# A hand-written instruction order of a retention and channel-mix kernel, replaced by another

## The chip, the cores and the metric

One core of one Trainium2 chip. The metric is the device time of one execution in microseconds (us). A run of the profiler gives, for one execution, every instruction of the five engines: TensorE (PE, with its weight loads as PEld), VectorE (DVE), ScalarE (ACT), GpSimd (POOL) and SyncE (SP).

## The reference

Inputs q, k, v of 4 batches x 8 heads x 768 tokens x 64, and a mixing layer with weights w_k (512 x 1024), w_v (1024 x 512), w_r (512 x 512) and vectors mu_k, mu_r. First a retention with decay, then the channel mix on its output:

```python
for t in range(S):
    state = gamma * state + outer(k[t], v[t])     # per batch and head, 64 x 64
    y[t] = scale * q[t] @ state
x = y, heads side by side                          # 4 x 768 x 512
xk = mu_k * x + (1 - mu_k) * x_prev                # x_prev: x one token earlier
xr = mu_r * x + (1 - mu_r) * x_prev
out = sigmoid(xr @ w_r) * (relu(xk @ w_k) ** 2 @ w_v)
```

## The kernel before, in words

The 3072 tokens are 12 blocks of 256, three to a batch: block n is part n % 3 of batch n // 3. For each block the kernel computes the retention in chunks, transposed, and puts the result in xT (512 features by tokens); then the channel mix of the block, or of two blocks together (GROUPS joins 3 with 4, 6 with 7 and 9 with 10).

A block is computed in one of three ways. Blocks in WIDE use two chunks of 128 tokens with full 128-row matmuls, blocks in HALF four chunks of 64 tokens in quarters of the array (64 x 64), and blocks 0 and 1 two chunks of 128 in pieces of 64 rows. Blocks in WHOLE transpose 128 x 64 pieces, the others 64 x 64 pieces.

Nothing schedules the program: the string ORDER is its order, on all engines at once. Each word is one step, `code.block.part`, with `~v`, `~a`, `~p`, `~s` naming the engine that does it (VectorE, ScalarE, GpSimd, SyncE) and `@` the PSUM banks that it uses. Each engine runs its own words in this order, one after the other, and waits for its inputs; so a word that waits holds up all later words of its engine. The words, in the order of a block:

- lq, lk, lv load q, k and v (lines 224 to 239). Those from `~p` are GpSimd's, which converts q and k to f16 on the way; the first halves of q and k of block 0 come from `~s` as f32 and are converted by cq and ck (cast, L248).
- vs scales v by the decay (scale_v, L254, instruction L255). Tq, Tk transpose q and k on TensorE (L274 whole, L280 in halves); Eq, Ek copy the result out of PSUM (copy, L243 on ScalarE).
- S are the scores (L320, L333, L341), M multiplies them by the mask on VectorE (L349, L356).
- C makes the state's increments (L368, L386, L397), U adds them up (L421, or a copy L245 for the first of a batch), G decays the state to the next block (L426 on ScalarE, L430 else).
- I and J bring the earlier state in (L443), Y the chunk's own tokens (L464, L480, L491), and D multiplies by gy, the powers of the decay, into xT (L509, L516).
- dx is the difference of neighbouring tokens (L531), X.n.w.j mixes 128 features for xk (w = 0) or xr (w = 1) (L560).
- K multiplies by w_k (L574 for two blocks, L584 for one), Qa and Qb are ReLU and square on ScalarE (L593, L601, L605), R multiplies by w_r (L614), s is the sigmoid (L620), V multiplies by w_v (L626, two words of four matmuls), O multiplies both into the output tile (L632), st stores it (L639).
- For the last 128 tokens of block 11, V, O and st come as Vc, Oc and sc in pieces of columns (L644, L651, L659).
- Once: gy.0 and gy.1 make the powers (L708 to L720), mu starts the loads of mu_k and mu_r on ScalarE's queue (load_mu, L676), mt transposes them on TensorE (L681), me copies them out on ScalarE (L684), wk, wr, wv load the weights in GpSimd's queue.
- z.n runs n units of matmuls on zeros that nobody reads, filler on TensorE: for each whole four units one f32 matmul (L693), for each one left over an f16 matmul of 512 columns (L700).

Tiles are in rings: 4 of q, k and v (f32 for v), 3 of most others, so a load also waits until its tile is free. GpSimd has at most eight loads under way.

Of the kernel before, what the change touches and what calls it, by code (L numbers as in the profile page):

```python
# [34 lines left out]
J.2 X.1.1.1 Qb.1.0 Qb.1.2 X.1.1.2 X.1.1.3 S.3.1@23 lv.4~p K.1.3@0 Qa.1.3 Qb.1.3 wv.0~p X.0.1.3
X.0.1.2 R.0.0@1 D.2~v dx.2~v X.2.0.2 Qb.0.1 s.0.0 X.2.0.0 lq.6~p R.0.1@6 s.0.1 Tk.4@0 X.2.0.3
R.1.1@7 X.2.0.1 vs.3~p M.3.0~v Ek.4~a K.2.3@1 Qa.2.3 K.2.0@6 Qa.2.0 M.3.1~v S.4.1@45 M.4.1~v
Tq.5@1 Eq.5~a C.3@23 U.3.0~v U.3.1 s.1.1 vs.4~v R.1.0@6 s.1.0 G.3~a K.2.1@0 I.3@45 Qb.2.3 S.4.0@23
M.4.0~v Y.3 C.4@67 U.4.0 U.4.1 G.4~a K.2.2@1 Qb.1.1 I.4@23 J.3 Qa.2.1 Qa.2.2 Y.4 Qb.2.0 D.3~v
V.0.0.0@6 Tq.6@45 J.4 dx.3~v V.1.1.0@7 D.4~v dx.4~v X.3.0.1 V.0.1.0@0 V.1.0.0@1 X.2.1.2 Qb.2.2  # L40
wv.1~p V.0.0.1 Eq.6~a V.0.1.1 lq.7~p lk.6~p Tk.6@45 Ek.6~a O.0.0 Tq.7@23 Eq.7~a V.1.0.1 S.6@45
lk.5~p Tk.5@6 X.3.0.2 X.3.0.3 X.3.0.0 K.3.3@2 Qb.2.1 K.3.2@3 O.1.0 Ek.5~a O.0.1 X.3.1.1 M.6~v
lv.5~p vs.5~v K.3.5@0 Qa.3.5 Qa.3.3 K.3.4@6 V.1.1.1 Qa.3.2 lv.6~p C.5@01 S.5@45 Qa.3.4 vs.6~v
C.6@23 Qb.3.3 Qb.3.2 O.1.1 M.5~v U.5.0 X.2.1.3 U.5.1 U.6.0~a U.6.1 U.6.2 U.5.2 U.6.3 K.3.0@6
X.2.1.1 Qa.3.0 Qb.3.0 V.2.0.0@7 K.3.6@4 Qa.3.6 K.3.7@6 st.0.1 Qa.3.7 Qb.3.7 I.5@01 I.6@45 V.2.0.1
K.3.1@3 Qa.3.1 Qb.3.1 X.2.1.0 R.2.0@6 lk.8~p Tk.8@23 lv.7~p Y.5 X.3.1.0 vs.7~v X.3.1.3 Y.6 X.3.1.2
s.2.0 R.3.1@6 D.5~v dx.5~v st.1.1 st.0.0 Ek.8~a X.5.0.3 O.2.0 X.5.0.0 V.2.1.0@2 X.5.0.1 R.3.0@3
D.6~v G.6~a Qb.3.4 s.3.0 s.3.1 lv.8~p R.2.1@0 s.2.1 X.5.1.3 X.5.0.2 R.4.0@1 s.4.0 V.2.1.1 lk.7~p
C.7@67 O.2.1 lk.9~p Tk.9@01 Ek.9~a lv.11~s Tk.7@45 Ek.7~a lq.8~p U.7.0 U.7.1 U.7.2 st.2.0 vs.8~v
K.5.1@3 dx.6~v Qa.5.1 K.5.2@2 I.7@45 S.7@01 U.7.3 K.5.0@6 M.7~v lv.9~p Qb.3.6 Qa.5.0 K.5.3@3  # L50
Qa.5.2 Qb.5.0 R.4.1@6 lk.11~p Qb.3.5 vs.9~v V.4.1.0@7 X.5.1.1 C.8@01 Y.7 D.7~v dx.7~v X.6.0.3
X.6.0.0 lq.11~p Qa.5.3 Qb.5.2 Tq.8@23 X.6.0.2 V.4.1.1 s.4.1 V.4.0.0@6 Eq.8~a V.3.1.0@2 Qb.5.3
Qb.5.1 V.4.0.1 X.6.0.1 lq.9~p G.7~a V.3.0.0@3 V.3.1.1 V.3.0.1 U.8.0 K.6.3@4 Qa.6.3 O.4.0 K.6.1@5
Qa.6.1 Qb.6.1 K.6.2@6 Qa.6.2 lq.10~p O.3.1 U.8.1 st.1.0 X.5.1.0 X.5.1.2 lk.10~p U.8.2 I.8@01 O.3.0
st.2.1 Tq.9@23 Eq.9~a O.4.1 Qb.6.3 S.8@45 M.8~v K.6.0@7 K.6.6@6 Qa.6.0 Qb.6.0 Qa.6.6 X.6.1.3
S.9@23 st.3.1 Tq.11@45 Y.8 Eq.11~a X.6.1.2 R.5.1@7 s.5.1 K.6.7@6 Qb.6.2 K.6.4@4 Qa.6.4 M.9~v D.8~v
dx.8~v X.8.0.0 X.8.0.3 X.8.0.1 X.8.1.1 V.5.0.0@5 R.5.0@7 K.6.5@4 s.5.0 X.6.1.1 Tk.10@01 Qa.6.7
lv.10~p vs.10~v X.6.1.0 C.9@23 U.9.0~v Ek.10~a st.3.0 Tq.10@67 V.5.0.1 O.5.0 X.8.0.2 V.5.1.0@0
R.6.1@1 Qa.6.5 U.9.1 U.9.2 U.9.3 Eq.10~a V.5.1.1 st.5.0 O.5.1 s.6.1 Qb.6.4 S.10@45 I.9@67 C.10@23
G.9~a vs.11~v U.10.0 U.10.1 U.10.2 Qb.6.5 M.10~v st.5.1 R.6.0@1 s.6.0 R.7.0@0 s.7.0 K.8.1@1 Qa.8.1  # L60
K.8.2@2 Qa.8.2 C.11@01 I.10@45 U.10.3 Y.9 K.8.0@3 D.9~v Qb.6.7 K.8.3@2 st.4.1 Tk.11@67 G.10~a
U.11.0 U.11.1 Qa.8.0 Ek.11~a U.11.2 Y.10 D.10~v R.7.1@3 s.7.1 dx.9~v dx.10~v X.9.1.1 I.11@01
X.8.1.0 S.11@67 M.11~v X.9.0.0 Qb.8.2 V.7.0.0@4 Qa.8.3 X.9.0.2 X.9.0.1 V.7.1.0@5 V.6.0.0@3 X.9.0.3
Qb.8.1 Qb.6.6 V.6.1.0@2 V.7.1.1 X.8.1.2 V.7.0.1 V.6.0.1 V.6.1.1 K.9.5@6 K.9.7@7 Qb.8.0 st.4.0
Qa.9.5 O.6.0 Y.11 O.7.1 X.8.1.3 R.8.1@6 D.11~v dx.11~v Qa.9.7 Qb.9.7 K.9.3@5 Qb.9.5 X.11.1.3
X.11.0.1 O.6.1 X.9.1.3 V.8.1.0@7 X.9.1.2 V.8.0.0@3 X.11.0.2 st.6.1 K.9.4@0 Qa.9.4 Qb.9.4 K.9.6@1
Qa.9.6 K.9.0@2 X.9.1.0 K.9.2@0 Qa.9.2 Qb.8.3 X.11.0.3 Qb.9.2 X.11.0.0 Qa.9.3 X.11.1.0 K.9.1@1
R.9.1@0 Qa.9.1 Qb.9.1 X.11.1.2 V.8.0.1 K.11.1@5 O.7.0 Qa.11.1 R.8.0@4 V.8.1.1 Qb.9.3 s.8.0
R.10.0@5 K.11.0@1 st.6.0 Qa.9.0 Qb.9.0 st.7.1 K.11.2@2 st.7.0 R.9.0@4 Qa.11.0 Qb.9.6 Qb.11.0
Qb.11.1 X.11.1.1 O.8.0 K.11.3@1 s.9.1 V.9.1.0@3 V.10.1.0@0 s.8.1 O.8.1 st.8.1 R.11.1@6 V.9.0.0@7  # L70
# [719 lines left out]
```

## Time and profile before

| | us |
|---|---|
| median of 3 runs | 156.06 (155.8 to 156.61) |
| the profiled execution | 156.68 |
| its span, first to last instruction | 154.9 |
| TensorE's first matmul starts | 1.05 |
| TensorE's last matmuls (L644 x8) start | 150.25 |
| the last store is issued | 151.78 |
| GpSimd scales v.1 (vs.1), v.3 (vs.3) | 11.00 for 1.94, 36.97 for 1.90 |

How to read the profile: busy time is given by engine; a line such as `L632 DVE ... x23 | 15.4, 683 | 14.5 <-ACT rs L620 7.4` is a group of 23 instructions of line 632 on VectorE, busy 15.4 us together, 683 ns each, before which the engine sat idle 14.5 us, 7.4 of it until a result of L620. In a timeline a row is start, busy time, engine, line, operation, tiles, shape and count, and in brackets the idle time before it with what ended it ("issue": nothing that the profile shows). The 40 slices give the busy share in tenths. TensorE's granted clock is 1.00 over the whole span by the core's view.

### The profile page before, as it was taken

The numbers are of one execution on the slowest core, as the hardware profiler recorded it, in microseconds if no ns is written. First come the engines' busy times: TensorE is split into PE (matmuls) and PEld (weight loads), VectorE is DVE, ScalarE is ACT, GpSimd is POOL, SyncE is SP. The second block draws the span as 40 slices with busy tenths as digits, with TensorE's granted clock in tenths as the row PEclk, the third lists the DMA queues.
The fourth block names the chain that finished last, engine by engine and source line by source line (L and its number), as shares of the span: only waits on it lengthen the run. The fifth ranks groups of instructions, "written<-read, shape, count | busy, mean of one in ns | idle before, by whom it ended". The sixth has DMA issues, their size and how long they took to land.

```text
span 154.9 us, 5520 instructions
## 1 busy us (share of the span) xinstructions
PE 146.0 (94%) x2423; PEld 83.9 (54%) x2423; DVE 126.9 (82%) x205; ACT 99.4 (64%) x186; POOL 55.5 (36%) x65
## 2 busy tenths in 40 slices
PE   7779799999999999999999999999999999999990
...
DVE  2588999999899999999999999998999998110541
...
DMA packets 45768, 22.31 MB, mean 144 GB/s; under 512 B 37416, under 2 KB 41392, under 8 KB 45744
## 3 DMA queue, kind: packets, MB, share of 16 engines
...
q8 instruction: 19, 0.31, 0.9%
...
## 4 chain that ended last, share of the span: by engine, by line
PE 55%; DVE 24%; DMA 12%; issue 4%; POOL 3%; DVEq 0%; POOLq 0%
PE ps L626 19%; DMA v<-in_v_dram 12%; PE ps L614 9%; PE ps L574 9%; PE ps L584 8%; DVE a L356 3%; DVE xk L560 3%; DVE xr L560 3%; DVE vs L255 3%; DVE dx L531 2%; DVE xT L516 2%; DVE tg L421 2%; DVE os L632 2%; PE ps L443 2%; DVE a L349 1%
## 5 line engine op out<-in xcount | busy, mean ns | idle before, releaser
L626 PE MATMUL ps<-wv,k2s 128*128 128x512 f16 x184 | 43.4, 379 | 0.0
L593 ACT ACTIVATE kr<-ps 128x512 f32<-128x512 f32 x48 | 27.8, 596 | 23.1 <-PE ps L574 18.0
L626 PEld LDWEIGHTS <-k2s 128*128 128x128 f16 x184 | 17.4, 98 | 20.0
L632 DVE SCALAR_TENSOR_TENSOR os<-ps,rs 128x512 f32<-128x512 f32 x23 | 15.4, 683 | 14.5 <-ACT rs L620 7.4
L614 PE MATMUL ps<-wr,xr 128*128 128x512 f16 x96 | 24.1, 380 | 0.0
L584 PE MATMUL ps<-xk,wk 128*128 128x256 f16 x192 | 24.0, 273 | 0.0
L232 POOL DMA_DIRECT2D k<-in_k_dram x20 | 17.7, 898 | 15.2 <-PE ps L280 10.5
L574 PE MATMUL ps<-xk,wk 128*128 128x512 f16 x96 | 22.5, 379 | 0.0
L584 PEld LDWEIGHTS <-wk 128*128 128x128 f16 x192 | 18.1, 98 | 4.9 <-DMA wk<-in_moe_w_k_dram 0.6
L620 ACT ACTIVATE rs<-ps 128x512 f32<-128x512 f32 x24 | 13.7, 594 | 9.3 <-PE ps L614 8.9
L560 DVE SCALAR_TENSOR_TENSOR xr<-dx,mu,xT 128x256 f16<-128x256 f32 (+1 forms) x36 | 19.2, 564 | 0.1
L560 DVE SCALAR_TENSOR_TENSOR xk<-dx,mu,xT 128x256 f16<-128x256 f32 (+1 forms) x36 | 18.8, 567 | 0.2
L232 POOL DMA_DIRECT2D v<-in_v_dram x18 | 16.2, 915 | 1.4 <-DMA q<-in_q_dram 0.5
L243 ACT COPY kT<-ps 128x1024 f16<-128x1024 f16 (+1 forms) x13 | 12.2, 947 | 5.2 <-PE ps L280 4.1
L601 ACT ACTIVATE k2s<-kr 128x512 f16<-128x512 f32 x24 | 14.9, 628 | 0.3
L574 PEld LDWEIGHTS <-wk 128*128 128x128 f16 x96 | 9.2, 98 | 10.8
L531 DVE TENSOR_TENSOR dx<-xT 128x1024 f32<-128x1024 f32 x12 | 14.6, 1223 | 0.3
L605 ACT ACTIVATE k2s<-kr 128x512 f16<-128x512 f32 x24 | 14.5, 628 | 0.1
L243 ACT COPY qT<-ps 128x1024 f16<-128x1024 f16 (+1 forms) x13 | 12.3, 949 | 2.4 <-PE ps L274 2.2
L614 PEld LDWEIGHTS <-xr 128*128 128x128 f16 x96 | 8.8, 97 | 9.2 <-DVE xr L560 0.2
L255 DVE TENSOR_TENSOR vs<-v,csm_sb 128x1024 f16<-128x1024 f32 x10 | 12.1, 1216 | 2.0 <-DMA v<-in_v_dram 2.0
L356 DVE TENSOR_TENSOR a<-ps,c_sb 128x1024 f16<-128x1024 f32 (+1 forms) x12 | 12.2, 1040 | 0.5 <-PE ps L333 0.4
...
## 6 DMA issues: line engine op xcount, KB each, us to landing
...
wk<-in_moe_w_k_dram POOLq DMA_DIRECT2D x2, 512.0 KB, 11.0
...
```

The costliest lines, as they stand in the source:

```text
L232: e.dma_start(out=dst[:, :, i * D : i * D + D], in_=src[:, i * P : i * P + P].rearrange("h p d -> p h d"),)
L243: e.copy(out=out, in_=in_)
L255: e.tensor_tensor(out=VS(n), in0=V32(n).rearrange("p h (i d) -> p i h d", i=2), in1=gks[:, int(half(n) or wide(n)), :, :, None].to_broadca ...
L356: nc.vector.tensor_tensor(out=a_full(n)[:, i, :, j0:j1], in0=pairs(banks("S", n, i, j0))[:, :, j0:j1], in1=(below if wide(n) else causal[: ...
L531: e.tensor_tensor(out=DX(k)[:, :, m * TM + t0 : m * TM + t1], in0=x[:, :, c + t0 : c + t1], in1=x[:, :, c - 1 + t0 : c - 1 + t1], op=ALU.s ...
L560: nc.vector.scalar_tensor_tensor(out=XM[w](k)[:, j, t0:t1], in0=DX(k)[:, j, t0:t1], scalar=mu[:, w * NCO + j : w * NCO + j + 1], in1=x[:, ...
L574: nc.tensor.matmul(banks("K", n, g), lhsT=wk16[:, co, g * P : g * P + P], rhs=XM[0](k)[:, co, :], start=(co == 0), stop=(co == NCO - 1),)
L584: nc.tensor.matmul(pz[:, i, :], lhsT=wk16[:, co, fo * P : fo * P + P], rhs=XM[0](k)[:, co, m * TM + t0 : m * TM + t1], start=(i == 0 and c ...
L593: nc.scalar.activation(out=kr, in_=banks("K", n, g, *u), func=AF.Relu)
L614: nc.tensor.matmul(banks("R", n, tb), lhsT=XM[1](k)[:, co, t : t + P], rhs=wr16[:, co, :], start=(co == 0), stop=(co == NCO - 1),)
L626: nc.tensor.matmul(banks("V", n, tb), lhsT=K2(n)[:, fo, tb * P : tb * P + P], rhs=wv16[:, fo, :], start=(fo == 0), stop=(fo == NFO - 1),)
L632: nc.vector.scalar_tensor_tensor(out=OS(2 * n + tb), in0=banks("V", n, tb), scalar=1.0 / (KSC * KSC), in1=RS(2 * n + tb), op0=ALU.mult, op ...
```

## The change

The constants and the whole order are replaced:

- block 5 leaves HALF and joins WIDE: 128-token chunks in place of 64-token ones; 64-token chunks are now used from block 6 on.
- all twelve vs are VectorE's; vs.1 and vs.3 were GpSimd's.
- U.0.0, U.3.0, U.9.0 and cq go from VectorE to ScalarE, G.7 from ScalarE to VectorE; all v loads are GpSimd's (lv.11 was SyncE's).
- the fillers are placed anew: before z.12, z.2, z.1, z.1, z.4, z.1, z.1; after z.3 four times ahead of the first transpose, then z.3, z.1, z.3, z.5, z.3, z.9.
- the first load on SyncE is k, then q (before: q, then k), the first on GpSimd half of k.0 (before: v.0). The words for mu come after cq on ScalarE.
- the last tile is cut in columns 256, 128 and 128 (CUTS) instead of 256 and 256; the order of the pieces is columns 256 to 383, then 0 to 255, then 384 to 511, the last stored from ScalarE's queue.

```diff
-HALF = (5, 6, 7, 8, 9, 10, 11)
+HALF = (6, 7, 8, 9, 10, 11)
...
-WIDE = (2, 3, 4)
+WIDE = (2, 3, 4, 5)
 HEADS = ((0, 1), (3, 2), (4, 5), (7, 6))
+CUTS = ((0, 256), (256, 384), (384, 512))
 ORDER = """
-lq.0.0.2~s gy.0 lv.0~p lk.0.0.2~s ck.0.0.2~v mu lk.0.2.4~p lq.0.2.4~p gy.1~a lv.1~p lk.1~p lq.1~p
-cq.0.0.2~v lq.2~p wk.0~p z.12@6 Tk.0.0.2@0 Tq.0.0.2@1 Ek.0.0.2~a Eq.0.0.2~a mt@2 wk.1~p vs.0~v
-z.2@6 S.0.0.0.2@01 me M.0.0.0.2~v S.0.1.0.2@45 Tk.0.2.4@2 M.0.1.0.2~v Tq.0.2.4@3 lk.2~p C.0@67
-U.0.0~v Ek.0.2.4~a Eq.0.2.4~a z.1@0 S.0.0.2.4@23 M.0.0.2.4~v I.0@45 S.0.1.2.4@01 M.0.1.2.4~v z.1@2
-Y.0 U.0.1 G.0~a vs.1~p Tk.1@7 Ek.1~a D.0~v dx.0~v lv.2~p lq.3~p lk.3~p C.1@01 U.1.0 X.0.0.0
-X.0.0.3 Tq.1@6 Eq.1~a z.4@2 S.1.1@67 lq.4~p X.0.0.2 I.1@45 Tq.2@0 M.1.1~v S.1.0@23 Eq.2~a wr~p
-X.0.0.1 z.1@7 K.0.0@6 M.1.0~v U.1.1 G.1~a lk.4~p Qa.0.0 X.0.1.0 X.0.1.1 Qb.0.0 Y.1 D.1~v dx.1~v
-X.1.0.1 z.1@3 K.0.3@7 X.1.0.2 Qa.0.3 K.0.2@1 X.1.0.0 Qa.0.2 X.1.0.3 Tk.2@6 K.0.1@0 Ek.2~a vs.2~v
-S.2.0@67 S.2.1@45 M.2.0~v Qb.0.3 K.1.1@1 K.1.2@2 Qa.0.1 Qb.0.2 lv.3~p C.2@0 Qa.1.2 Tq.3@3 Eq.3~a
...
-s.11.0 Oc.11.1.1 sc.11.1.1~a O.11.0 st.11.0 V.10.0.1 O.10.0 st.10.0 Vc.11.1.0@0 Oc.11.1.0
-sc.11.1.0~s
+lk.0.0.2~s lk.0.2.4~p gy.0 ck.0.0.2~v lq.0.0.2~s lv.0~p lq.0.2.4~p z.3@6 z.3@6 z.3@6 z.3@6
+Tk.0.0.2@0 Tk.0.2.4@1 vs.0~v cq.0.0.2~a Tq.0.0.2@2 lv.1~p mu Ek.0.0.2~a Eq.0.0.2~a z.3@6
+S.0.1.0.2@23 M.0.1.0.2~v Ek.0.2.4~a mt@0 me S.0.0.0.2@45 M.0.0.0.2~v Tq.0.2.4@1 C.0@67 Eq.0.2.4~a
+S.0.0.2.4@01 U.0.0~a I.0@23 M.0.0.2.4~v S.0.1.2.4@45 M.0.1.2.4~v vs.1~v z.1@0 Y.0 gy.1~a D.0~v
+U.0.1 lq.1~p Tq.1@6 Eq.1~a lk.1~p lk.2~p dx.0~v X.0.0.0 wk.0~p z.3@0 Tk.1@2 Ek.1~a X.0.0.2 X.0.0.1
+G.0~a X.0.0.3 z.5@0 Tk.2@2 X.0.1.2 C.1@67 Ek.2~a U.1.0 U.1.1 G.1~a S.1.1@45 M.1.1~v lv.2~p z.3@0
+I.1@23 S.1.0@01 M.1.0~v K.0.1@7 vs.2~v Qa.0.1 K.0.0@6 Y.1 wk.1~p z.9@4 K.0.3@7 K.0.2@0 Qa.0.0
+Qb.0.0 Qa.0.2 lq.2~p Tq.2@6 C.2@1 D.1~v dx.1~v Eq.2~a X.1.0.1 X.1.0.3 X.1.0.0 X.1.0.2 K.1.2@2
...
+st.9.1 s.11.0 st.9.0 Oc.11.1.1 st.10.1 sc.11.1.1~s V.11.0.1 O.11.0 st.11.0 Vc.11.1.0@7 Oc.11.1.0
+sc.11.1.0~s Vc.11.1.2@2 Oc.11.1.2 sc.11.1.2~a
 """
...
     def values_c(e, n, tb, c):
-        x = slice(c * dm // 2, (c + 1) * dm // 2)
+        x = slice(*CUTS[c])
```

The same line is replaced in result_c and store_c. The lines of the changed kernel stand one below those given here (CUTS adds a line).

More of the change, by code (lines that the diff above doesn't have):

```diff
@@ L35 @@
[L35 to L70, printed above, removed]
@@ L71 @@
-Qa.11.3 V.11.0.0@1 s.10.0 Qa.11.2 Qb.11.2 R.10.1@2 V.9.1.1 O.9.1 V.10.1.1 s.10.1 O.10.1 st.9.1
-Qb.11.3 V.9.0.1 st.10.1 s.11.1 Vc.11.1.1@2 s.9.0 V.10.0.0@6 O.9.0 R.11.0@0 V.11.0.1 st.8.0 st.9.0
-s.11.0 Oc.11.1.1 sc.11.1.1~a O.11.0 st.11.0 V.10.0.1 O.10.0 st.10.0 Vc.11.1.0@0 Oc.11.1.0
-sc.11.1.0~s
+lk.0.0.2~s lk.0.2.4~p gy.0 ck.0.0.2~v lq.0.0.2~s lv.0~p lq.0.2.4~p z.3@6 z.3@6 z.3@6 z.3@6
+Tk.0.0.2@0 Tk.0.2.4@1 vs.0~v cq.0.0.2~a Tq.0.0.2@2 lv.1~p mu Ek.0.0.2~a Eq.0.0.2~a z.3@6
+S.0.1.0.2@23 M.0.1.0.2~v Ek.0.2.4~a mt@0 me S.0.0.0.2@45 M.0.0.0.2~v Tq.0.2.4@1 C.0@67 Eq.0.2.4~a
@@ new lines @@
+S.0.0.2.4@01 U.0.0~a I.0@23 M.0.0.2.4~v S.0.1.2.4@45 M.0.1.2.4~v vs.1~v z.1@0 Y.0 gy.1~a D.0~v
[3 more added lines that the diff above has]
+Qb.0.0 Qa.0.2 lq.2~p Tq.2@6 C.2@1 D.1~v dx.1~v Eq.2~a X.1.0.1 X.1.0.3 X.1.0.0 X.1.0.2 K.1.2@2
+Qa.0.3 X.1.1.0 X.1.1.3 S.2.0@45 Qa.1.2 Qb.1.2 U.2.0 S.2.1@01 X.0.1.1 Qb.0.2 I.2@67 K.1.1@3 Qa.1.1
@@ new lines @@
+Qb.1.1 M.2.0~v lq.3~p K.1.0@2 lk.3~p Tk.3@4 M.2.1~v Y.2 Tq.3@3 Qb.0.1 Ek.3~a X.1.1.2 Eq.3~a wr~p
+J.2 X.0.1.0 X.0.1.3 R.0.1@5 Qa.1.0 X.1.1.1 Qb.0.3 D.2~v s.0.1 R.1.0@0 dx.2~v X.2.0.3 X.2.0.2
+lq.4~p lk.4~p X.2.0.1 S.3.0@67 X.2.0.0 s.1.0 S.3.1@23 M.3.1~v lv.3~p Tk.4@4 Ek.4~a Tq.4@1 Eq.4~a
+R.0.0@5 lk.5~p s.0.0 K.2.2@0 Qa.2.2 vs.3~v K.2.0@4 Qa.2.0 S.4.1@23 M.3.0~v Tk.5@5 Ek.5~a C.3@01
+U.3.0~a M.4.1~v K.1.3@4 lv.4~p R.1.1@6 Qb.1.0 s.1.1 U.3.1 lq.5~p Qa.1.3 vs.4~v I.3@23 S.4.0@01
+M.4.0~v K.2.3@5 G.3~a C.4@67 Tq.5@4 Qa.2.3 U.4.0 U.4.1 wv.0~p Y.3 lq.7~p Eq.5~a X.2.1.0 I.4@01 J.3
@@ new lines @@
+D.3~v Y.4 S.5.0@45 M.5.0~v wv.1~p Qb.1.3 V.1.0.0@7 Tq.7@23 lk.7~p dx.3~v G.4~a J.4 V.0.0.0@6 D.4~v
+dx.4~v Qb.2.2 Eq.7~a X.3.0.3 X.3.0.1 K.2.1@4 X.3.0.0 V.0.1.0@5 V.1.0.1 O.1.0 V.0.1.1 X.3.0.2 O.0.1
+Qa.2.1 Qb.2.1 V.1.1.0@4 Tk.7@01 Ek.7~a lq.6~p lv.5~p Tq.6@23 Eq.6~a vs.5~v V.0.0.1 O.0.0 V.1.1.1
+K.3.4@7 Qa.3.4 X.2.1.1 lk.6~p K.3.6@0 lv.6~p Qa.3.6 X.2.1.3 C.5@5 Qb.2.0 Tk.6@23 Ek.6~a Qb.3.6
+S.5.1@67 U.5.0 X.2.1.2 K.3.5@1 O.1.1 R.2.0@5 Qb.2.3 K.3.0@0 M.5.1~v I.5@23 vs.6~v s.2.0 Qa.3.5
+Qa.3.0 S.6@67 S.7@45 M.7~v M.6~v Y.5 K.3.3@1 C.6@45 U.6.0~a U.6.1 Qb.3.5 Qa.3.3 Qb.3.3 lv.7~p J.5
@@ new lines @@
+vs.7~v K.3.7@0 U.6.2 D.5~v lv.9~p U.6.3 K.3.1@6 Qa.3.1 dx.5~v Qa.3.7 lq.8~p X.5.0.2 X.5.0.1 Qb.3.7
+st.0.1 R.2.1@7 lq.9~p lk.10~p s.2.1 X.5.0.0 K.3.2@1 Qa.3.2 st.1.1 V.2.0.0@4 G.6~a X.5.0.3 I.6@23
+C.7@67 lv.8~p U.7.0 U.7.1 Tq.8@01 Eq.8~a X.3.1.1 Qb.3.4 Qb.3.2 U.7.2 V.2.1.0@5 V.2.0.1 lk.9~p
+st.0.0 O.2.0 K.5.2@0 Qa.5.2 U.7.3 V.2.1.1 Qb.5.2 I.7@01 O.2.1 st.2.1 K.5.3@6 K.5.1@4 Qb.3.0 Qb.3.1
+V.4.0.0@5 X.3.1.3 X.5.1.1 lv.10~p Qa.5.3 Qb.5.3 Qa.5.1 Tk.9@67 Ek.9~a lk.8~p Y.7 st.2.0 Y.6
+X.3.1.0 X.3.1.2 R.4.0@4 R.4.1@6 s.4.1 vs.8~v V.4.0.1 D.6~v D.7~v V.3.1.0@7 s.4.0 O.4.0 dx.6~v
```

24 lines of the change are left out of this document (22 added, 2 removed).

## The prediction

> **What bounds the kernel now.** I read the page's busy shares first, then its 40 slices, then TensorE's timeline, then VectorE's, each with what ended the idle time.
>
> ```profile
> PE 146.0 (94%) x2423; PEld 83.9 (54%) x2423; DVE 126.9 (82%) x205; ACT 99.4 (64%) x186; POOL 55.5 (36%) x65
> ...
> PE   7779799999999999999999999999999999999990
> ...
> DVE  2588999999899999999999999998999998110541
> ```
>
> PE is full from the eleventh slice to the last; it ends at 151.3, and 3.6 us of last result, store and closing follow. VectorE is full from slice three until about 131 us. So the end is TensorE's work plus the waits between 1.05 us (its first instruction) and 151.3. VectorE sets the pace of the start, where TensorE can only do what VectorE has made.
>
> The timeline of TensorE (start, busy, line, count, idle before and its releaser):
>
> ```profile
> 7.58 0.20 PE L681 MATMUL ps<-csm_sb,mu 8*128 8x8 f32 x1 [0.84 <-DMA mu<-in_moe_mu_r_dram]
> ...
> 15.59 0.35 PE L341 MATMUL ps<-qT,kT 64*64 64x128 f16 x10
> 16.29 0.30 PE L341 MATMUL ps<-qT,kT 64*64 64x128 f16 x6 [0.34 <-issue]
> ...
> 18.42 1.10 PE L584 MATMUL ps<-xk,wk 128*128 128x256 f16 x8
> 19.73 0.64 PE L491 MATMUL ps<-a,vs 64*64 64x128 f16 x32 [0.21 <-DVE a L356]
> ...
> 24.79 1.95 PE L584 MATMUL ps<-xk,wk 128*128 128x256 f16 x16
> ...
> 27.75 0.31 PE L443 MATMUL ps<-qT,tg 64*64 64x128 f16 x8 [0.33 <-DVE tg L421]
> ...
> 38.92 0.44 PE L386 MATMUL ps<-vs,k 128*64 128x64 f16 x16 [0.52 <-POOL vs L255]
> ```
>
> The second pair is the wait for instructions that the change is after: S.1.1 is one group of 16 with one input, it stops after ten, and nothing releases it. It costs about 0.55 us. Queue q8 (instruction) shows 19 packets and 0.31 MB for 2 x 2423 TensorE instructions, that is 256 instructions a packet; I find no second stop inside a group that only such a packet explains. So at most 0.6 us is to be had from it.
>
> **Spacings.** Start to start, from the timeline and the chain of waits: 0.216 us for a 512-column matmul (4 in 0.86), 0.109 for 256 columns (8 in 0.87), 0.57 for a whole transpose word (16), 0.27 for a half one (32), 0.33 for a wide scores word of 8 with its change of shape; going from dense to small work adds 0.09, back again 0.12 to 0.15. Counting both orders word by word with these gives, from the first K.1 word (24.79 us now) to the last matmul, 124.3 us of work now. Measured are 126.5; the 2.2 left over are waits, the largest 0.4 at 27.75, 0.6 at 38.92, 0.3 at 58.1 and 0.3 at 75.1. The count is good to 0.2 us.
>
> **Part 1, filler.** The z words hold 22 units now and 36 after. Now they last 5.1 (z.12, at the slow first clock, 0.85 a pass), 1.1 (z.4) and 6 x 0.216: 7.5 us. After: four z.3 ahead of the first transpose, which at the same slow rate are again about 5.1; 12 units at 0.216, 2.6; three of the f32 kind in z.5 and z.9 at 1.06 (z.4's row), 3.2. Together 10.9, or 3.4 us more TensorE time. Filler is free where TensorE would have waited anyway, so the start has to be followed on VectorE.
>
> **Part 2, VectorE's start.** Its timeline now:
>
> ```profile
> 8.16 1.23 DVE L255 TENSOR_TENSOR vs<-v,csm_sb 128x1024 f16<-128x1024 f32 x1 [2.00 <-DMA v<-in_v_dram]
> ...
> 13.02 1.23 DVE L516 TENSOR_TENSOR xT<-ps,gy_sb 128x1024 f32<-128x1024 f32 x1 [0.52 <-PE ps L443]
> ...
> 20.91 1.23 DVE L516 TENSOR_TENSOR xT<-ps,gy_sb 128x1024 f32<-128x1024 f32 x1
> ```
>
> D.0 starts at 13.02 and D.1 at 20.91. After, POOL issues half of k.0 ahead of v.0; k's landing now follows v's by about 0.4 (Tk.0.2.4 starts at 8.61, vs.0 at 8.16), so v.0 comes 0.4 later and vs.0 starts near 8.6. Four half masks (0.6 each) follow, and then vs.1 (1.13), which was POOL's (1.94 at 11.00): D.0 at 8.6 + 1.13 + 2.4 + 1.13 + 0.2 = 13.45 at the earliest, even though U.0.0 (0.4) goes to ScalarE.
>
> From D.0 to the end of M.1.0 VectorE does D.0 1.26, two U before the masks and one after D.0 at 0.335 each, dx 1.26, five X at 0.395, two masks 2.26: 7.8 us, against 6.7 now, where one U and one X come later. So Y.1 is at 21.3 at the earliest, against 19.73. TensorE has its fillers, Tq.1, Tk.1, Tk.2, C.1 and two K.0 words in that time and waits little; two K.0 words are done by Y.1 instead of one.
>
> From Y.1 to the first K.1 word TensorE needs 5.6 us: Y.1 0.6, z.9 2.4, two K.0, Tq.2, C.2. VectorE's vs.2, D.1, dx.1 and four X need 5.3 in parallel. So z.9 costs only 0.3; without it the X would be waited for. First K.1 word: 26.9 at the earliest.
>
> **Part 3, mu.** Now ScalarE issues both mu loads in its first 2.6 us:
>
> ```profile
> 1.73 0.58 ACTq L676 DMA_DIRECT2D mu<-in_moe_mu_k_dram  x1
> 2.34 0.27 ACTq L676 DMA_DIRECT2D mu<-in_moe_mu_r_dram  x1
> ```
>
> mt (L681) still waited until 7.5: 5.1 us from the second issue. After, cq.0 is a ScalarE copy ahead of them, waiting for q from SP (now second on SP; SP's second load was in by 5.2, when ck started). So the second mu issue is at about 5.85. mt stands in TensorE's order behind S.0.1.0.2, near 9, and everything queued behind it waits: S.0.0.0.2, Tq.0.2.4 and C.0, and on ScalarE, behind me, Eq.0.2.4, without which the last two scores, their masks, vs.1 and D.0 don't come. From mt to M.0.0.2.4 I count 1.75 us (S 0.3, T 0.25, 0.2 to ScalarE, copy 0.6, S and its change 0.3, 0.1); VectorE is free for that mask at 10.9. So mu is harmless up to 9.2 and costs VectorE a microsecond for each one after.
>
> The latency at this time is not shown. Nearest rows: the page's csm_sb load on the same queue 2.4 us, mu itself 5.1, a v load on SP's queue among others 6.4; so mu is in between 8.3 and 12.3. I start from mu's own row and take 0.7 off, since c_sb (issued at 1.19, 3.2 to landing) stood ahead of it on ScalarE's queue until 4.4: 4.4 us, mu in at 10.2, loss 1.0, range 0 to 3.1.
>
> [...]
>
> So the first K.1 word is at 27.9.
>
> **Part 4, the rest.** From there the new order holds 124.9 us: 0.35 more because S.2 (0.65) comes after that point and C.2 (0.3) before it, 0.2 because block 5 in 128-token chunks has dearer scores (16 x 27 ns for 32 x 8.5) and dearer intra matmuls, the rest shape changes. VectorE's whole load grows by about 1.4 us: vs.1 and vs.3 +2.26, second mask of block 5 +1.13, G.7 +0.34, against cq 0.4, three U to ScalarE 1.0, two U and a split D of block 5 0.9. That is hidden: I laid VectorE's sum beside TensorE's sum from 28 us on; the closest K, R, I, Y or C word has its input 0.4 us early, most over 1. So the waits of now (2.2) should go, POOL's scaling at 38.92 among them; I leave 0.3, between 0 and 1.2, for copies on ScalarE.
>
> Last tile: Vc pieces of 256, 128, 128 columns in place of 256, 256. 16 matmuls of 128 columns are not in the trace; bounds are half of 0.109 (no change) and 0.109 itself (+0.85); I take +0.2, as nearer to half, since weight loads (98 ns) overlap in the 256-column row. [...] The last result covers 128 columns: 0.29 (the 128-column row of gy_sb) for 0.42, and half the bytes: -0.2 (0 to -0.4).
>
> **Sum.** Last matmul: 27.9 + 124.9 + 0.3 + 0.2 = 153.3, against 151.3: +2.0; tail -0.2; so +1.8. The profiled run took 156.68 (span 154.9), so 158.5; the median of the runs is 156.06, 0.6 lower, so **157.9** beside it. 0.5%, or 0.8 us, is about what a measurement of this kernel can tell from no change.
>
> **Rivals** (times beside the median).
> 1. **mu in time (chance 0.25: within 0.5%).** A small load needs 2.4 us as csm_sb did, and mt waits for nothing. Then the first K.1 word is at 26.9 and the time 156.9; with no late waits and 128 columns at half of 256, 156.4. For it: csm_sb's row. Against: mu's own. [...]
> 2. **More than one wait for instructions (0.17: faster).** The waits view puts some 8 us of TensorE's weight loads down to "issue" (L280 1.5, L341 1.3, L491 1.1, L368 1.1 and so on). I took them for changes of shape, which the new order has as often (79 against 80). If those before 45 us are instructions that come late, the new order, which has fewer instructions in front of each packet and filler between, saves up to 1.5 of them; with mu in time that is 157.9 - 1.0 - 1.5 = 155.4. It decides if the gaps at changes of shape shrink by half before 45 us. Against: the same idle of 0.42 stands before L280 at 45.38 and 50.29, where TensorE's own loss is only 0.09.
> 3. **VectorE waits for v.3 (0.08: slower).** POOL now idles 3.6 us before its scaling of v.3, which starts at 36.97 when v.3 lands. VectorE is in order; its vs.3 is due near 38. If v.3 comes after 39.2 (C.3 has 1.2 to spare), each microsecond is lost: 2 us late beyond that, 160.
>
> That the instruction wait stays is inside the range (0.55).
>
> Forecast 0.50: 157.0 to 159.4 on its own. With the rivals the range is **155.3 to 160.0**; about a tenth is left out at each end. Faster 0.17, same 0.25, slower 0.58.
>
> **What would show it.** Right: L681 released by mu after 9.5; D.0 after 13.5 and D.1 after 22.3; the first K.1 word after 27; TensorE's waits after 28 us under 1; no stop inside a scores group. Wrong: D.1 before 22, or waits for DVE or ACT of over 1 us after 30; then the end follows those and not this sum.

## The result, and the profile after

The changed kernel takes 160.12 us in the median of four runs (159.96 to 161.51), the kernel before on the same chip 156.28 (155.80 to 156.61): a ratio of 1.026, 95% interval 1.021 to 1.031. Slower was forecast, at 157.9 us; the time is 2.2 us above that and just outside the range. The profiled execution took 161.51 us, span 159.7; it is the slowest of the four, the others lie between 159.96 and 160.17. (Executions over 1.5% above the fastest of their kernel are left out of every ratio but not out of the medians, so the two can differ a little.)

The page of the changed kernel: busy time, then the 40 slices of some 4 us each. The clock's row is new here, since it stood at 9 throughout before.

```profile
PE 150.9 (94%) x2383; PEld 85.9 (54%) x2383; DVE 128.1 (80%) x203; ACT 100.2 (63%) x186; POOL 53.5 (34%) x65
...
PE   7928999999999999989999998999999999999992
...
DVE  2367969999999999998978999999999999120252
...
PEclk9995599999999999999999999999999999999999
```

TensorE's third slice is nearly empty (a 2), and right behind it two slices run at half the granted clock (the two 5s). TensorE is busy 4.9 us longer than before with 40 instructions fewer: longer filler in part, a lower clock for the rest. In the eighteenth slice (67.9 to 71.9 us, an 8) it stops once more.

TensorE's timeline of the start, then VectorE's, then what ScalarE's queue issued for mu:

```profile
10.87 0.20 PE L682 MATMUL ps<-csm_sb,mu 8*128 8x8 f32 x1 [2.82 <-DMA mu<-in_moe_mu_r_dram]
...
15.30 1.07 PE L275 MATMUL ps<-c_sb,q 128*64 128x128 f16 x16
...
20.30 0.64 PE L275 MATMUL ps<-c_sb,k 128*64 128x128 f16 x16
...
21.14 0.40 PE L342 MATMUL ps<-qT,kT 64*64 64x128 f16 x16
...
24.73 0.64 PE L492 MATMUL ps<-a,vs 64*64 64x128 f16 x32
...
29.98 1.05 PE L585 MATMUL ps<-xk,wk 128*128 128x256 f16 x8
```

```profile
8.16 1.23 DVE L256 TENSOR_TENSOR vs<-v,csm_sb 128x1024 f16<-128x1024 f32 x1 [2.85 <-DMA v<-in_v_dram]
...
11.35 0.69 DVE L357 TENSOR_TENSOR a<-ps,c_sb 128x512 f16<-128x512 f32 x1 [1.37 <-PE ps L342]
...
15.47 1.23 DVE L517 TENSOR_TENSOR xT<-ps,gy_sb 128x1024 f32<-128x1024 f32 x1 [0.30 <-issue]
...
25.72 1.22 DVE L517 TENSOR_TENSOR xT<-ps,gy_sb 128x1024 f32<-128x1024 f32 x1
```

```profile
5.13 0.55 ACTq L677 DMA_DIRECT2D mu<-in_moe_mu_k_dram  x1
5.70 0.27 ACTq L677 DMA_DIRECT2D mu<-in_moe_mu_r_dram  x1
```

Read them together. mt (L682) waits for mu until 10.87; mu's second load was issued at 5.70, so it was 5.17 us from issue to use (5.24 in the kernel before, 2.34 to 7.58). VectorE's second mask (11.35) waited for the scores queued behind mt, so D.0 starts at 15.47 in place of 13.02, D.1 at 25.72 in place of 20.91, and the first K.1 word at 29.98 in place of 24.79. The two transpose rows are the clock: 16 transposes take 1.07 us at 15.30 and 0.64 at 20.30. The scores word S.1.1 (21.14), which stopped after ten before, is now one piece of 16: the stop that the change was after has gone from there. (That it was a wait for instructions is the author's reading; the row of before shows 0.34 us that nothing releases.) The new order need not be the reason, since two variants of the old order below (only mu, or only mt and me moved) don't show that stop either.

The windows view puts numbers to it: a stretch, its length, then busy time of PE, PEld, DVE, ACT and POOL with counts, granted clock, DMA share, GB/s.

```profile
9.18:12.59 3.41, 1.42 (x57) 1.03 (x57) 1.50 (x3) 1.07 (x4) 2.53 (x3) 1.00 1.81 179
12.59:16.00 3.41, 3.14 (x67) 2.32 (x65) 2.95 (x4) 1.12 (x4) 2.43 (x3) 0.50 1.70 193
16.00:19.42 3.42, 3.42 (x28) 1.73 (x25) 3.38 (x7) 1.64 (x2) 1.69 (x3) 0.50 1.14 250
19.42:22.83 3.41, 3.41 (x96) 1.80 (x95) 2.11 (x6) 2.74 (x8) 1.92 (x3) 1.00 1.57 190
```

TensorE worked 1.42 us of the first stretch, and the next two, 6.83 us together, were granted half the clock. In the profile of before the clock is never halved inside the span (mean 1.000; after, 0.978).

After 28 us there is one stop of the kind that the change was to remove, inside the group of 32 C matmuls of block 7:

```profile
70.62 0.38 PE L369 MATMUL ps<-vs,k 64*64 64x64 f16 x20
71.66 0.28 PE L369 MATMUL ps<-vs,k 64*64 64x64 f16 x9 [0.66 <-issue]
```

Three of the 32 ran just ahead, among those of the word before; nothing releases the 24th. That is 0.66 us of idle time, about 0.85 against the spacing of the others.

### The profile page after: what moved, and what is told of

Read it like the earlier page. It is cut to its first block, busy times and chain, and to the rows that moved or that the text cites. A ratio compares the mean times of both kernels' runs of the same rounds, so it can differ in the third digit from the quotient of the medians.

```text
span 159.7 us, 5450 instructions
## 1 busy us (share of the span) xinstructions
PE 150.9 (94%) x2383; PEld 85.9 (54%) x2383; DVE 128.1 (80%) x203; ACT 100.2 (63%) x186; POOL 53.5 (34%) x65
## 4 chain that ended last, share of the span: by engine, by line
PE 84%; DVE 6%; DMA 6%; issue 1%; ACT 1%; SPq 0%; DVEq 0%
PE ps L627 25%; PE ps L615 13%; PE ps L585 13%; PE ps L575 11%; PE ps L275 4%; DMA mu<-in_moe_mu_r_dram 3%; DMA k2s<-in_q_dram 2%; PE ps L444 2%; PE ps L281 2%; PE ps L694 2%; PE ps L334 2%; PE ps L701 2%; DVE a L357 1%; DVE xr L561 1%; PE ps L481 1%
## 5 line engine op out<-in xcount | busy, mean ns | idle before, releaser
L627 PE MATMUL ps<-wv,k2s 128*128 128x512 f16 x184 | 44.4, 379 | 0.0
L575 PE MATMUL ps<-xk,wk 128*128 128x512 f16 x96 | 23.4, 379 | 0.0
L233 POOL DMA_DIRECT2D v<-in_v_dram x20 | 18.1, 937 | 9.4 <-DVE vs L256 6.7
L256 DVE TENSOR_TENSOR vs<-v,csm_sb 128x1024 f16<-128x1024 f32 x12 | 14.6, 1219 | 2.9 <-DMA v<-in_v_dram 2.9
L357 DVE TENSOR_TENSOR a<-ps,c_sb 128x1024 f16<-128x1024 f32 (+1 forms) x14 | 14.6, 1067 | 2.1 <-PE ps L342 2.1
## 6 DMA issues: line engine op xcount, KB each, us to landing
wv<-in_moe_w_v_dram POOLq DMA_DIRECT2D x2, 512.0 KB, 10.2
```

The source lines that it names most:

```text
L233: e.dma_start(out=dst[:, :, i * D : i * D + D], in_=src[:, i * P : i * P + P].rearrange("h p d -> p h d"),)
L256: e.tensor_tensor(out=VS(n), in0=V32(n).rearrange("p h (i d) -> p i h d", i=2), in1=gks[:, int(half(n) or wide(n)), :, :, None].to_broadca ...
L357: nc.vector.tensor_tensor(out=a_full(n)[:, i, :, j0:j1], in0=pairs(banks("S", n, i, j0))[:, :, j0:j1], in1=(below if wide(n) else causal[: ...
L575: nc.tensor.matmul(banks("K", n, g), lhsT=wk16[:, co, g * P : g * P + P], rhs=XM[0](k)[:, co, :], start=(co == 0), stop=(co == NCO - 1),)
L627: nc.tensor.matmul(banks("V", n, tb), lhsT=K2(n)[:, fo, tb * P : tb * P + P], rhs=wv16[:, fo, :], start=(fo == 0), stop=(fo == NFO - 1),)
```

## The experiments

Theory A, after the result: all of the loss comes from mt. It stands early in TensorE's order, mu comes 5.2 us after a late issue, and this costs twice, once because VectorE's masks come late (about 2 us) and once because 3 us of idle TensorE halve its clock for 6.8 us (about 1.5 us). Rivals: B, the new order with its extra VectorE work and filler is slower by itself; C, the clock has nothing to do with it.

**mu early.** The changed kernel with the two loads of mu issued ahead of the casts.

```diff
-lk.0.0.2~s lk.0.2.4~p gy.0 ck.0.0.2~v
+lk.0.0.2~s lk.0.2.4~p gy.0 mu ck.0.0.2~v
...
-Tq.0.0.2@2 lv.1~p mu Ek.0.0.2~a
+Tq.0.0.2@2 lv.1~p Ek.0.0.2~a
```

> The changed kernel with one word moved: mu is issued as ScalarE's first own word, as it was before, and no longer behind cq.0. Theory A (mu's late issue holds TensorE for 3 us at mt, and that idle time is what halves the granted clock from 12.6 to 19.4 us): mt is released before 8.5, the clock stays 1.0, D.0 starts at 13.5, the first K.1 word at 27, the median near 157.0 (3 us less than 160.1). Rival B (VectorE's longer list decides, the start of it does not matter): D.0 earlier, but the end within 0.8 us of 160.1. Rival C (the clock falls for another reason, such as too little work in the first 12 us whatever mt does): the clock is halved again in about the same stretch, median 158.5 or more.

Measured: 156.38 us median (155.39 to 158.09, ten runs), ratio to before 0.9985 (0.995 to 1.002). TensorE's timeline:

```profile
7.88 0.22 PE L682 MATMUL ps<-csm_sb,mu 8*128 8x8 f32 x1
...
26.78 1.05 PE L585 MATMUL ps<-xk,wk 128*128 128x256 f16 x8
```

mt starts at 7.88 and waits for nothing; D.0 is at 12.87, the first K.1 word at 26.78. The clock was not full in this profile: its mean over the 154.9 us is 0.989, which is 3.4 us at half, and 16 transposes take 1.07 us at 12.69. The five runs with a mean clock of 0.997 or more took 155.4 to 156.4. So where mu is issued is worth 3.7 us, and B in its strong form is out.

**The same delay put into the kernel before.** Only the word mu moves, behind gy.1.

```diff
-ck.0.0.2~v mu lk.0.2.4~p lq.0.2.4~p gy.1~a lv.1~p
+ck.0.0.2~v lk.0.2.4~p lq.0.2.4~p gy.1~a mu lv.1~p
```

> The kernel before with one word moved: mu is issued on ScalarE behind gy.1, at about 5.5 us and not at 1.7. Theory A: mu lands near 10.8, mt holds TensorE from 6.5 on, over 4 us, the clock is halved for a window of 6.8 us after it, D.0 starts at 15 to 15.5, and the median is 159 to 161 (3 to 5 us more than before). Rival B (an early loss is made good later because TensorE's queue has slack): within 1 us of 156.3. Rival C (the clock fell in the changed kernel for its other fillers): no halved clock here, +2 us.

Measured: 161.42 us (160.94 to 163.72, four runs), ratio 1.033 (1.028 to 1.038). TensorE's timeline, and the windows view as above:

```profile
11.21 0.24 PE L681 MATMUL ps<-csm_sb,mu 8*128 8x8 f32 x1 [4.22 <-DMA mu<-in_moe_mu_r_dram]
```

```profile
6.16:9.57 3.41, 0.82 (x17) 0.48 (x16) 1.23 (x1) 1.55 (x4) 3.41 (x5) 1.00 1.38 251
9.57:12.99 3.42, 1.78 (x21) 0.78 (x23) 0.10 (x1) 0.17 (x1) 3.11 (x4) 0.50 1.75 183
```

The late mu alone makes the old order as slow as the new one, without any of the other edits. With the longer idle of 4.2 us (6.99 to 11.21) come three halved stretches, 10.24 us, from 9.57 to 19.81, that is from inside the wait on; the mean clock is 0.968.

**mt late.** The changed kernel with mu as late as it is there, but mt and me moved down the order, behind the last scores of block 0.

```diff
-Ek.0.2.4~a mt@0 me S.0.0.0.2@45
+Ek.0.2.4~a S.0.0.0.2@45
...
-vs.1~v z.1@0 Y.0 gy.1~a
+vs.1~v z.1@0 mt@0 me Y.0 gy.1~a
```

> The changed kernel with mu's late issue kept, but mt and me moved behind the last scores of block 0, just ahead of Y.0, where mu has landed. Theory A: TensorE waits under 0.3 us at mt, the clock stays at 1.0, D.0 at 13.5, median 156.9 to 157.3, as for the early issue. Rival D (the late mu load itself slows the other first loads, not the wait for it): 158.5 or more.

Measured: 156.42 us (156.00 to 158.67, ten runs), ratio 1.002 (0.998 to 1.006). TensorE's timeline, then VectorE's:

```profile
11.18 0.22 PE L682 MATMUL ps<-csm_sb,mu 8*128 8x8 f32 x1
...
26.04 1.05 PE L585 MATMUL ps<-xk,wk 128*128 128x256 f16 x8
```

```profile
12.81 1.23 DVE L517 TENSOR_TENSOR xT<-ps,gy_sb 128x1024 f32<-128x1024 f32 x1 [0.26 <-ACT gy_sb L712]
```

mt starts even later than in the changed kernel (11.18 for 10.87), and the 3.7 us are gone: D.0 is at 12.81. What cost the time was the work queued behind mt, not that mu came late. The clock stayed full in this profile (mean 0.998). It did not in all runs: five of the ten have a mean clock of 0.978 to 0.989, that is one or two halved stretches, and three of these five took 156.38 to 156.54 us, like the runs at full clock (156.00 to 156.57).

**Filler in the wait.** The changed kernel, mt and mu where they are, with twelve more matmuls on zeros ahead of mt.

```diff
-Ek.0.2.4~a mt@0 me S.0.0.0.2@45
+Ek.0.2.4~a z.3@0 z.3@0 z.3@0 z.3@0 mt@0 me S.0.0.0.2@45
```

> The changed kernel with 12 more units of zero matmuls (2.6 us) between S.0.1.0.2 and mt, so that TensorE is busy while mu is awaited; mt still comes at 10.9. It tells the wait from the clock. Theory A: the clock stays at 1.0, D.0 at 15.0, Y.1 at 22.9 and not 24.7, the first K.1 word at 28.4, median 158.5. If all of the loss is the late mt and none the clock: 160. If all of it is the clock: 157.

Measured: 158.64 us (157.93 to 159.21, four runs), ratio 1.016 (1.010 to 1.022). The timeline, then the same stretch by windows:

```profile
7.89 2.76 PE L701 MATMUL ps<-zero 128*128 128x512 f16 x12
10.75 0.20 PE L682 MATMUL ps<-csm_sb,mu 8*128 8x8 f32 x1
...
28.18 1.05 PE L585 MATMUL ps<-xk,wk 128*128 128x256 f16 x8
```

```profile
8.47:11.88 3.41, 3.31 (x60) 1.67 (x58) 1.81 (x3) 0.48 (x2) 3.28 (x5) 1.00 1.61 199
11.88:15.29 3.41, 2.41 (x78) 1.73 (x74) 2.71 (x5) 1.71 (x6) 2.84 (x4) 1.00 1.89 180
```

mt is about as late as in the changed kernel (10.75 for 10.87), but TensorE was busy meanwhile, the clock stayed at 1.00, and 1.5 us of the time came back (160.12 to 158.64). This separates the two prices: against the kernel with mt late (156.42), 2.2 us are the late scores, and 1.5 us the halved clock. The split is good to some 0.6 us: the four runs lie in two pairs, 157.93 and 158.11, 159.18 and 159.21, all at full clock, and what parts them is not known; all four are below all four of the changed kernel. The first K.1 word says much the same: 26.04, 28.18 and 29.98 in the three kernels, steps of 2.1 and 1.8. C is out.

**mt late in the kernel before.** Is the 0.84 us wait for mu in the kernel before worth anything?

```diff
-Eq.0.0.2~a mt@2 wk.1~p
+Eq.0.0.2~a wk.1~p
...
-z.2@6 S.0.0.0.2@01 me M.0.0.0.2~v
+z.2@6 S.0.0.0.2@01 M.0.0.0.2~v
...
-M.0.1.2.4~v z.1@2
+M.0.1.2.4~v z.1@2 mt@2 me
```

> The kernel before with mt and me moved behind the last scores of block 0; mu is issued early as it was. Its trace shows TensorE idle for 1.05 us ahead of mt. Theory P (VectorE's chain from vs.0 sets the start, and that idle time lies under the wait for v.0 until 8.2): the same as before within 0.3 us. Theory Q (TensorE's own work sets it): 0.7 to 1.0 us less, 155.5.

Measured: 156.23 us (155.93 to 159.19, twelve runs), ratio 0.999 (0.997 to 1.0005). Nothing: there the wait lay beside VectorE's own wait for v.0 (vs.0 at 8.27).

**Without most of the filler.** The mt-late kernel without the fillers behind the first transposes (z.3, z.1, z.3, z.5, z.3, z.9); the first four stay.

```diff
-Ek.0.0.2~a Eq.0.0.2~a z.3@6
+Ek.0.0.2~a Eq.0.0.2~a
...
-wk.1~p z.9@4 K.0.3@7
+wk.1~p K.0.3@7
```

> e3_mt_late without the fillers behind the first transposes (z.3, z.1, z.3, z.5, z.3, z.9: 24 units, about 5.8 us of TensorE); the four z.3 at the start stay. Theory A1 (the granted clock is decided by how busy TensorE was in a stretch of some 3.4 us, and the fillers keep it): the clock is halved for one or more stretches of 3.4 us between 8 and 26, and the median is 157 to 159. Theory A2 (only a gap of about 3 us in one piece halves it): the clock stays at 1.0 and the median is 156.1 to 156.4, since z.9 alone stood in the way, by 0.3.

Measured: 157.13 us (156.84 to 157.73, seven runs), ratio 1.0055 (1.003 to 1.008). The clock's row of the slices, and the K.1 word in TensorE's timeline:

```profile
PEclk9995569999999999999999999999999999999999
```

```profile
27.45 0.78 PE L585 MATMUL ps<-xk,wk 128*128 128x256 f16 x4 [1.43 <-DVE xk L561]
```

The clock was halved for 10.24 us (12.17 to 22.41), longer than in the changed kernel, yet only 0.7 us is lost against the mt-late kernel (0.5 by the ratios). All seven runs have a mean clock of 0.964 to 0.989, against five of ten with filler: the filler does help to keep the clock, and all in all it is worth about 0.7 us here. That is not the price of the slow clock alone, since some 5.8 us of matmuls left with the filler, and in this start TensorE has slack where VectorE sets the pace.

**Can the mended order be made faster?** Six kernels start from the mt-late one. First, vs.1 goes back to GpSimd (and v.2's load is issued earlier).

```diff
-M.0.1.2.4~v vs.1~v z.1@0 mt@0 me Y.0 gy.1~a D.0~v
+M.0.1.2.4~v z.1@0 mt@0 me Y.0 gy.1~a D.0~v
...
-X.0.0.0 wk.0~p z.3@0 Tk.1@2
+X.0.0.0 wk.0~p lv.2~p vs.1~p z.3@0 Tk.1@2
...
-M.1.1~v lv.2~p z.3@0
+M.1.1~v z.3@0
```

> e3_mt_late with vs.1 back on GpSimd (behind the loads of v.2, so that those keep their place; wk's second half is then issued a microsecond later). The prediction held vs.1 on VectorE to cost the start, as 1.13 us stand ahead of D.0. In e3's trace Y.0 on TensorE ends only 0.4 before vs.1 does, so: D.0 at 12.4 and not 12.8, the median 0.2 to 0.5 below e3's 156.4. If VectorE's load as a whole counts (theory V): 1.0 below. If it counts nowhere: the same within 0.2; if wk's second half or vs.1 itself comes late: above.

Measured: 157.09 us (156.13 to 158.82, twelve runs), ratio 1.003 (1.001 to 1.006), no gain. VectorE's timeline says why:

```profile
12.87 1.23 DVE L517 TENSOR_TENSOR xT<-ps,gy_sb 128x1024 f32<-128x1024 f32 x1 [1.40 <-ACT gy_sb L712]
```

VectorE is free 1.40 us earlier and D.0 stands where it stood: it now waits for gy.1, which ScalarE does behind me. A freed engine met the next limit.

Second, that kernel with mu early too, one X behind M.1.0, and z.9 cut to z.1.

```diff
-gy.0 ck.0.0.2~v
+gy.0 mu ck.0.0.2~v
...
-lv.1~p mu Ek.0.0.2~a
+lv.1~p Ek.0.0.2~a
...
-Tk.2@2 X.0.1.2 C.1@67
+Tk.2@2 C.1@67
...
-M.1.0~v K.0.1@7 vs.2~v
+M.1.0~v X.0.1.2 K.0.1@7 vs.2~v
...
-wk.1~p z.9@4
+wk.1~p z.1@4
```

> A try at a better version: e5's order with mu issued early as well, X.0.1.2 moved behind the masks of block 1 (0.4 less on VectorE ahead of Y.1) and z.9 cut to z.1. By the sums of the prediction, the first K.1 word comes 0.4 + 0.4 + 0.3 earlier than in e3: 155.3. If the cut filler costs a stretch of clock, or wk's second half is then waited for: 156 to 157.

Measured: 157.15 us (155.52 to 159.67, twelve runs), ratio 1.001 (0.998 to 1.004). D.0 13.24, again 1.40 us of idle VectorE for gy.1. With z.9 cut to z.1, TensorE waited 0.84 us for the second half of wk ahead of a K.0 word (22.73), which the expectation had named as a risk, and 0.70 for X ahead of the first K.1 word, which came at 26.05.

Three kernels then tried vs.2 (1.22 us of VectorE) behind D.1 and the filler between Y.1 and the K.0 words, together and apart.

```diff
-M.1.0~v K.0.1@7 vs.2~v Qa.0.1
+M.1.0~v K.0.1@7 Qa.0.1
...
-wk.1~p z.9@4
+wk.1~p z.5@4
...
-Tq.2@6 C.2@1 D.1~v
+Tq.2@6 D.1~v
...
-X.1.0.2 K.1.2@2 Qa.0.3
+X.1.0.2 vs.2~v K.1.2@2 C.2@1 Qa.0.3
```

> The order of e3_mt_late with two edits in the start: vs.2 (1.22 us of VectorE) moves from ahead of D.1 to behind the last X of block 1, with C.2, which needs it, moved behind the first K.1 word; and the filler between Y.1 and the K.0 words shrinks from z.9 (2.2 us) to z.5 (1.1 us). Theory V, the start is paced by VectorE and by filler sized to it, and the 1.25 us by which the first K.1 word of e3 (26.04 us) is later than that of before (24.79) is where the gain of the removed waits went: D.1 moves from 21.8 to 20.6, the first K.1 word from 26.04 to about 24.9, the last matmul from 151.1 to 150.0, and the time is about 155.3 us against 156.4 for e3, ratio to before 0.993 to 0.996. Rival W, the later order has no slack, so that work moved out of the start (vs.2, C.2) is waited for there: the first K.1 word at 24.9 as well, but waits of VectorE's results of 0.5 us or more between 25 and 40 us, and a time of 156 or more. Rival H, less filler lets the clock halve: a stretch of 3.41 us at half clock and a time of 156 to 157.

> The order of e3_mt_late with vs.2 behind the last X of block 1 and C.2 behind the first K.1 word, and the filler z.9 left as it is. Theory V, filler and VectorE both end together at the K.1 words: D.1 comes at 20.6, but TensorE still has its z.9 to do, so the first K.1 word moves only by the C.2 that left (0.3 us), to about 25.7, and the time is 156.1 to 156.5. If VectorE alone paced the start, K.1 would move by 1.1 and the time would be 155.3.

> The order of e3_mt_late with only the filler z.9 cut to z.5. Theory V: TensorE reaches the first K.1 word 1.1 us earlier and waits for VectorE's X there, so the first K.1 word stays at 26.0 within 0.2, with a wait of about 1 us before it released by VectorE, and the time is 156.2 to 156.6. If the filler alone delayed the start, K.1 would come at 24.9 and the time would be 155.3.

Measured: together 157.92 us (six runs, ratio 1.010, 1.007 to 1.014); vs.2 alone 158.67 (eight runs, 1.010, 1.006 to 1.013); the filler alone 156.79 (twelve runs, 1.005, 1.0015 to 1.008). VectorE's and TensorE's timelines of the first:

```profile
22.33 1.22 DVE L517 TENSOR_TENSOR xT<-ps,gy_sb 128x1024 f32<-128x1024 f32 x1 [0.93 <-PE ps L444]
```

```profile
27.71 0.32 PE L387 MATMUL ps<-vs,k 128*64 128x64 f16 x8 [0.32 <-DVE vs L256]
```

The theory behind them falls: D.1 (22.33) did not come at 20.6 but waited 0.93 us for TensorE's Y.1 and I.1, which stand behind VectorE's own masks of block 1, so vs.2 had been in a gap. Moved, it is late for C.2 instead (27.71). The first K.1 word came at 26.18 and not at 24.9. The rival, that the later order has no slack for it, is what happened to the time, though the waits between 25 and 40 us were 0.3 to 0.4 and not 0.5 or more. The profiles of the second and third have a mean clock of 0.978 over 157.1 and 156.4 us, which is some 6.9 us at half clock each; their first K.1 words, at 27.79 and 27.56, missed the expected 25.7 and 26.0, and with the clock halved they can't decide what those two moves are worth by themselves.

Last, gy.1 earlier on ScalarE, in the kernel with vs.1 on GpSimd; Y.0 also moves ahead of z.1 and mt, and z.5 is cut to z.1.

```diff
-U.0.0~a I.0@23
+U.0.0~a gy.1~a I.0@23
...
-z.1@0 mt@0 me Y.0 gy.1~a D.0~v
+Y.0 z.1@0 mt@0 me D.0~v
...
-z.5@0 Tk.2@2
+z.1@0 Tk.2@2
```

> The order of e5_vs1_gpsimd (mt behind the last scores of block 0, vs.1 on GpSimd) with gy.1 on ScalarE moved from behind me to right behind U.0.0, Y.0 moved ahead of z.1 and mt, and the filler z.5 cut to z.1. In e5 VectorE idled 1.40 us ahead of D.0 for gy.1, which is why taking vs.1 off VectorE gave nothing. Theory V2, gy.1 was the next limit and VectorE paces the rest of the start: D.0 moves from 12.9 to about 12.1, D.1 from 21.8 to about 21.1, the first K.1 word from 26.1 to about 25.4, and the time is 155.5 to 156.2, ratio to before 0.995 to 0.999. Rival F, TensorE (its transposes, its filler and its waits for loads) paces the start as much: D.0 comes early, but the first K.1 word stays within 0.3 of 26.1 and the time within 156.2 to 157.1. Rival H, less filler lets the clock halve for one or two stretches of 3.41 us: K.1 after 26.3 and 156.5 or more.

Measured: 155.94 to 159.52 us in six runs, median 158.86, before 156.18; too scattered for an interval. In the profiled run (156.52) D.0 came at 12.25, as expected, but the mean clock is 0.989 over 154.8 us, which is 3.4 us at half (16 transposes take 1.06 us at 12.82 and 0.64 at 15.20), and VectorE then waited for TensorE:

```profile
18.09 0.42 DVE L422 TENSOR_TENSOR tg<-ps,tg 128x256 f16<-128x256 f32 x1 [0.97 <-PE ps L398]
```

The first K.1 word came at 26.62, and not at 25.4: the rival that less filler lets the clock halve is what this profile shows. No version clearly beats the kernel before; the changed order with mu early or mt late equals it.

## Why the prediction was wrong in size

- **What bounds the kernel**: right. The start is paced by VectorE and TensorE in turn, the rest is TensorE's. (In the row shown, PE is at 9 from the sixth slice on, not from the eleventh; nothing hangs on it.)
- **Part 1, filler**: the four z.3 ahead of the first transpose were put at 5.1 us; they took 5.0 (1.06 to 6.06), 0.42 us for each 512-column matmul, twice the later 0.216. Right. That a slow first clock is the reason was not shown: the profile's clock row reads 9 there.
- **Part 2, VectorE's start**: the lengths hold. From D.0 to Y.1 7.85 us was forecast, the mt-late kernel has 7.98; from Y.1 to K.1 5.6 against 5.25. The base was 0.6 too late: vs.0 was put at 8.6 and started at 7.8 in the mt-late kernel, 8.1 with mu early and 8.16 in the changed kernel, so D.0 without a late mu is at 12.81, not 13.45.
- **Part 3, mu. This is the step that failed**, in two ways. The latency: "I start from mu's own row and take 0.7 off" gave 4.4 us; it was 5.17, and mu came at 10.87, not 10.2. The row (5.24, taken as 5.1) was right and the correction, argued from c_sb ahead in the queue, was not. That is 0.7 us. And "costs VectorE a microsecond for each one after" left out what the wait does to TensorE: with 2.82 us of idle time its clock was halved for 6.83 us, a term that the sum put at nothing; it is 1.5 us by the medians of the filler experiment. The prediction had the slow pace of the first filler in its sum (0.85 us a pass) and did not ask whether the new wait could slow TensorE again. 0.7 and 1.5 are the 2.2 us between 157.9 and 160.12, and that they close it so exactly is partly luck, as the split of the prices is good to 0.6 and smaller errors below cancel. With the clock kept, the filler kernel took 158.64; the forecast's own sum, with mt at its 10.75, is 157.9 + 0.55 = 158.45.
- **Harmless up to 9.2** was 0.6 too late for the same reason as D.0: in the filler kernel mt at 10.75 costs 2.15 us of D.0 (14.96 against 12.81), which puts the point at 8.6. The two errors of 0.6 cancel as soon as mu is late, so D.0 itself comes out (13.45 + 10.75 - 9.2 = 15.0).
- **Part 4, the rest**: 124.9 us from the first K.1 word to the last matmul, plus late waits. The mu-early kernel has 124.70, the filler kernel 124.76, mt late 125.02. Right. The changed kernel's profile has 126.34 (29.98 to 156.32): the stop at 71.0 (0.66) and a wait for VectorE near 97 (0.35) make 1.0 of the excess, and some 0.4 is spread. Late waits of 0.3 were too few for this execution, though within the range given, 0 to 1.2, by these two rows. The other three executions took 1.3 us or more less than the profiled one. GpSimd's scaling is waited for no more, as forecast.
- **Last tile**: the 128-column matmuls were put 0.2 us above half of the 256-column spacing. Eight of them take from 152.88 to 153.33, 0.056 us each: half of 0.109, no extra. From the start of the last matmul to the end of the span it is 3.4 us after and 3.9 before, so the tail shrank by 0.5 where 0.2 was taken.
- **Rivals.** *mu in time* did not happen, but its price was right: 156.4 to 156.9 forecast, 156.38 measured where mu is early. That its first K.1 word agrees as well (26.9 forecast, 26.78) is luck: it includes a halved stretch, and with mt late and the clock full it came at 26.04. *More than one wait for instructions* is refuted as far as the rows go: the later part took what the count with its shape changes gave. *v.3* was never waited for: vs.3 starts at 40.79 straight behind a mask, and C.3 behind it without a wait; in the mt-late kernel, where the start is not delayed, vs.3 starts at 36.85, again straight behind a mask.
- **The signs named** came: L682 released by mu after 9.5, D.0 after 13.5, D.1 after 22.3, K.1 after 27, no stop inside a scores group. TensorE's waits after 28 us, 0.66 and 0.35, are just not under 1 together.

Where did the intended gain go? With mt late, the new order needs 125.02 us from the first K.1 word to the last matmul, the kernel before 126.23 in its own profile and 125.52 in the one with mt late: 0.5 to 1.2 us less, since GpSimd's scaling and other waits are gone. But its first K.1 word is at 26.04, against 24.79 and 25.12: 0.9 to 1.25 us later, with scaling and filler put into a start that had no room. The two cancel; that this is the whole account was argued from the rows, and the kernels meant to win the start back did not.

One thing stays open: whether the new order can be free of such stops, and what they are. Stops inside a group that nothing releases appear in the changed kernel (0.66 us idle at 71.0) and in two of its variants (0.34 us with mt late and 0.83 with vs.1 on GpSimd, both at 81.5), and in none of the other profiles; the kernel before has its stop at 15.9, its two variants have none. What decides it was not tried.
